# The last eight parts of an FFT convolution: their constant matrices asked for early, stores moved to SyncE's queue, sums made in pairs

## The chip, the cores and the metric

The kernel runs on one core of a Trainium2 chip. The core has a matrix engine (TensorE, PE in the profile), a vector engine (VectorE, DVE), a scalar engine (ScalarE, ACT), GpSimd (POOL) and SyncE (SP), which here only issues transfers. All five run their own instruction lists and wait for each other through semaphores; transfers are issued from the lists of SP, ACT and POOL and carried out by 16 DMA engines. The metric is the device time of one execution in microseconds (us), lower is better.

## What is computed

The reference is one block of a network over 2048 positions and 640 channels, in float32. Cut to what matters:

```python
h = _layernorm(x) * (1 + ca) + sa
x = x + ga * ssm_conv(h)          # y = irfft(rfft(K) * rfft(h)) + h * Dskip, K from A, B, C, dt
h = _layernorm(x) * (1 + cb) + sb
x = x + gb * ((_silu(h @ w1) * (h @ w3)) @ w2)
```

The first half is a long convolution, done through a Fourier transform that is itself written as matrix products. The second half is an MLP with 1728 hidden channels, done in fp32r matrix products that are most of the kernel's time.

## The kernel before

**Stages.** The convolution's kernel `K` is made in 40 steps of 16 channels, and the transform runs beside it. The 640 channels are five chunks of 128 (`NDC`), and each chunk has eight parts (`g` = 0 to 7). I number the parts 0 to 39 over the chunks, n = 8*chunk + g, so that the last chunk is parts 32 to 39. One part goes through six pieces:

- `stage2`: 8 matmuls of the input and of `K` (tile `uk`) with a constant matrix `s2`, into a PSUM tile `p2`. The profile drops digits at the end of a name, so this is the group p<-uk,s. Two PSUM tiles serve the last parts by turns.
- `k_copy`: ACT copies the half of `p2` that belongs to `K` into `kc`.
- `products`: two DVE multiplications, T<-p,kc and p<-p,kc.
- `sums`: two DVE instructions, a subtraction and an addition of 128x256 each, into `Y` (two buffers).
- `inverse1`: 8 matmuls with a second constant matrix `i1` into a PSUM tile `pz`, the group pz<-Y,i. One `pz` holds two parts.
- `z_store` (`z_last` in the last chunk): ACT copies `pz` into a tile `zt`, and two transfers bring it to `zs` in DRAM.

**Constants.** `s2` and `i1` are different for each g, 256 KB each, and are loaded anew for every part into two buffers each (`stage2_load`, `inverse1_load`, on SP). A load can therefore start only when the part two before it has been through its matmuls.

**Order.** Up to step 40 the order of every engine is written out by hand (`FRONT`, `ROUND`). What is left, from the copy `kc` of part 32 on, is done by a plain loop, `for tk in range(NS + 1, LAG + 8 * NDC + 2)`, whose steps ask for stage2, k_copy and products and sums of one part and inverse1 and z_store of the part before it. There the order is not fixed by hand: the framework's scheduler orders each engine's list by what it expects to be ready. Only ACT's copies keep the order of the program (`acopy`), so that ACT's list is always kc(n), zt(n-1), kc(n+1), zt(n).

**What comes next.** `z_last` stores the last chunk part by part. While the last parts run, POOL loads `z` tiles back for the first four MLP row tiles (`z_load`, and the loads in `z_last` after parts 37 and 39), `x_part` turns them with small matmuls (py<-A,i) and adds the residual; after part 39 `x_first` finishes them, with 10 and 18 matmuls on an idle tile around it (`keep_warm`) that keep PE busy. Then the MLP starts. The MLP's hidden tiles are `h_tile()`, 18 places of 128x512 in the pool `xp`, which is opened in the space of the tables (`tabs`) after step 41. When the first weights of the MLP and two tiles of x are asked for hangs on `i1_last`, the last load of an `i1`.

Of the kernel before, what the change touches and what calls it, by code (L numbers as in the profile page):

```python
# [9 lines left out]
F32 = mybir.dt.float32  # L10
F32R = mybir.dt.float32r
I32 = mybir.dt.int32
AF = mybir.ActivationFunctionType
OP = mybir.AluOpType
# [3 lines left out]
P = 128  # L18
# [5 lines left out]
NDC = D // DC  # L24
SD = 16
SPC = DC // SD
NS = D // SD
EB = 4
NT = L // P
KD = D // P  # L30
# [83 lines left out]
def tile_kernel(ctx: ExitStack, tc: tile.TileContext, a):  # L114
    nc = tc.nc
    V, S, G, PE = nc.vector, nc.scalar, nc.gpsimd, nc.tensor
# [3 lines left out]
    zs = dram.tile([NDC, NB, 2, NA, DC], F32, name="zs")  # L120
# [15 lines left out]
    V, S, G, PE, Q = (InOrder(tc, e, (front,)) for e in (nc.vector, nc.scalar, nc.gpsimd, nc.tensor, nc.sync))  # L136

    def keep(ins):

        return tc.keep_in_program_order(ins) if in_order[0] else ins  # L140
# [5 lines left out]
    def acopy(out, in_):  # L146
        return tc.keep_in_program_order(S.copy(out, in_))
# [30 lines left out]
    tabs = ExitStack()  # L178
# [482 lines left out]

    ahead = {}

    def stage2_load(g):

        s2 = fp.tile([P, 4, P], F32, name="s2")
        nc.sync.dma_start(s2, a["s2"][:, g * 4:g * 4 + 4, :])
        return s2

    def inverse1_load(g):  # L670

        i1 = fp.tile([P, 2, 2, P], F32, name="i1")
        i1_last[0] = nc.sync.dma_start(i1, a["i1"][:, g * 2:g * 2 + 2])
        return i1

# [33 lines left out]
    def sums(ch, g):  # L709
        T, T2 = Pq.pop((ch, g))  # L710
        Y = fp.tile([P, 2, 2, DC], F32, name="Y")
        keep(V.tensor_tensor(Y[:, :, 0, :], T[:, :, 0, :], T2[:, :, 0, :], op=OP.subtract))
        last_sum[0] = keep(V.tensor_tensor(Y[:, :, 1, :], T[:, :, 1, :], T2[:, :, 1, :], op=OP.add))
        Yq[ch, g] = Y

    last_sum = [None]
# [34 lines left out]
    def z_last(g):  # L751

        zt = fp.tile([P, 8, DC], F32, name="zt", bufs=2)[:, :4]
        acopy(zt.rearrange("p (i r) d -> p r i d", r=2), Zq[NDC - 1][:, :, (g % 2) * 2:(g % 2) * 2 + 2, :])
        for c in range(2):
            (nc.sync if g == 7 and c else S).dma_start(zs[NDC - 1, :, c, g * 4:g * 4 + 4], zt[c * 64:c * 64 + 64])
        if g in (5, 7):
            fs = (0, 24) if g == 5 else (24, 32)
            for j in range(4):
                for c in range(2):  # L760
                    r = slice(c * 32 + fs[0], c * 32 + fs[1])
                    ins = (nc.gpsimd if g == 5 else S if c else nc.sync).dma_start(
                        early[j][1][64 + r.start:64 + r.stop, :, 2 * DC:], zsv[r, 4 * j:4 * j + 4, NDC - 1])
                    if g == 5 or c == 0:
                        zlast[g == 5] = ins


    def z_load(z, j, ks, q=nc.sync, b0=0):

        nb = z.shape[1]  # L770
        for k in ks:
            hh = int(k > 1)
            kk = k - 2 * hh
            q.dma_start(z[hh * 64:hh * 64 + 64, :, kk * DC:kk * DC + DC],
                        zsv[:, 4 * j + b0:4 * j + b0 + nb, k])

    def x_tile():
        return xp.tile([P, D], F32, name="xm", bufs=6)

    def h_tile():  # L780
        return xp.tile([P, 512], F32, name="h", bufs=18)
# [16 lines left out]
    early = []  # L798
# [6 lines left out]
    def x_part(j, after):  # L805

        x, z, st = early[j]
        py = [psS.tile([P, 512], F32, name="py", tag=t, bufs=1) for t in ("pk", "pb")]
        with tc.issue_after(after.ins):
            for b in range(4):  # L810
                for hh in range(2):
                    r, c = slice(hh * 64, hh * 64 + 64), slice(b * NA, b * NA + NA)
                    PE.matmul(py[hh][c, :2 * DC], i2[r], z[r, b, :2 * DC], start=True, stop=True,
                              tile_position=(r.start, c.start))
        S.copy(x[:, 512:], xe[j][:, 512:])
        for hh in range(2):
            h = slice(hh * 256, hh * 256 + 256)
            V.tensor_tensor(x[:, h], py[hh][:, :256], xe[j][:, h], op=OP.add)
        for k in range(4):
            V.bn_stats(st[:, k, :], x[:, k * P:(k + 1) * P])  # L820


    LAG = SPC + 2

    def conv_part(fn):
# [3 lines left out]
             "PQ": lambda k: exp_slow((k,)), "XQ": slow, "E1": real1, "E2": real2, "A1": imag1, "A2": imag2,  # L829
             "kg": kgen, "K": k1evac, "pt": k_stage1, "uk": k_out}  # L830
    conv = {"st": conv_part(stage2), "kc": conv_part(k_copy), "T": conv_part(products), "Y": conv_part(sums),
            "iv": conv_part(inverse1), "zt": conv_part(z_store)}
    by_two = ("PH", "AB", "CO", "SI")
    done = set()

    def do(name, k):

        lo, hi = (LAG, LAG + 8 * NDC) if name in conv else (0, NS)
        if name in by_two and k % 2:
            return None  # L840
        if front[0]:
            assert (name, k) not in done and lo <= k < hi, (name, k)
        if (name, k) in done or not lo <= k < hi or (name == "zt" and k % 2 == 0 and k < LAG + 8 * NDC - 8):
            return None
        done.add((name, k))
        return (conv if name in conv else parts)[name](k)
# [5 lines left out]
    fp = None  # L852
    xp = None
    first_w = dict.fromkeys(("wg", "wu"))

    def pre_end():

        pre.close()
        return ssm.enter_context(tc.tile_pool(name="fp", bufs=2, side="right", reuse_waits="tile"))
# [52 lines left out]
    for word in FRONT:  # L912
        name, k = word[:2].rstrip("+"), int(word[len(word[:2].rstrip("+")):])
        if name == "CL":
            fp = pre_end()
# [25 lines left out]
    for rnd in range(NS // EB):  # L941
        if 2 <= rnd < 7:
            late_load(rnd - 2)
        for word in ROUND:
            name, k = word[:2].rstrip("+-"), EB * rnd + int(word[len(word[:2].rstrip("+-")):])
# [11 lines left out]
    in_order[0] = False  # L957

    for tk in range(NS + 1, LAG + 8 * NDC + 2):
        do("st", tk)  # L960
        do("kc", tk)
        last = do("iv", tk - 1)
        do("zt", tk - 1)
        do("T", tk)
        do("Y", tk)
        if tk == NS + 1:
            tabs.close()
            xp = ctx.enter_context(tc.tile_pool(name="xp", bufs=2))
            idle = xp.tile([P, 512], F32R, name="idle", bufs=1)
            G.memset(idle.bitcast(F32), 0.0)  # L970
            for j in range(4):
                early[j] = (x_tile(), early[j][1], xp.tile([P, KD, 6], F32, name="st5", bufs=4))
        i = tk - 1 - LAG - 8 * NDC + 8
        if 0 <= i < 8:
            if i < 4:
                z_load(early[i][1], i, (3,), q=nc.gpsimd)
            for j in ((), (), (), (), (0,), (1,), (), (2, 3))[i]:
                x_part(j, last)
# [18 lines left out]
    V, S, G, PE = (InOrder(tc, e, (in_order,)) for e in (nc.vector, nc.scalar, nc.gpsimd, nc.tensor))  # L997
# [166 lines left out]
    ahead = {(0, n): w for n, w in first_w.items()}  # L1164
# [410 lines left out]
```

## Time and profile before

| | us |
|---|---|
| median of 3 runs | 952.9 (952.22 to 956.66) |
| the profiled execution | 954.98 |
| its span, first to last instruction | 952.8 |
| PE busy | 879.5 (92%) |
| DVE busy | 710.2 (75%) |
| ACT busy | 538.9 (57%) |
| stretch of the last eight parts: stage2 of part 32 starts, inverse1 of part 39 ends | 343.57 to 377.47 |

The profile's times count from the start of its span. PE, DVE, ACT, POOL are engines; SPq, ACTq and POOLq are instructions that issue a transfer. L108 is the line of the helper that records nearly all instructions, so groups are told apart by the tiles. A matmul of fp32 data is shown twice, so the 8 matmuls of a stage2 or an inverse1 are x16. The clock that PE was granted is 1.00 at full speed and 0.50 at half.

### The profile page before, as it was taken

How to read it: one execution, taken by the hardware profiler on the slowest of the kernel's cores; microseconds unless marked ns; L12 is line 12 of the kernel's file. 1: busy time of each engine (PE TensorE's matmuls, PEld its weight loads, DVE VectorE, ACT ScalarE, POOL GpSimd, SP SyncE). 2: the span in 40 equal slices, each digit the busy share in tenths (PEclk: the TensorE clock that was granted, in tenths of full speed). 3: DMA queues.
4: the chain of work that ended last, by engine and by line, in shares of the span. 5: the costliest groups of instructions: out<-in, count | busy, mean ns of one | idle time of the engine just before them, and what ended most of it. 6: DMA issues, size and time to landing. Idle time of an engine off the chain costs nothing.

```text
span 952.8 us, 20012 instructions
## 1 busy us (share of the span) xinstructions
PE 879.5 (92%) x7950; PEld 669.8 (70%) x7950; DVE 710.2 (75%) x1232; ACT 538.9 (57%) x737; POOL 269.0 (28%) x293
## 2 busy tenths in 40 slices
PE   3687979999998898999999999999999999999997
PEld 2453556666666664678888887578888888888786
DVE  5999979999999957577666665587976666664674
ACT  5877989999999632455333332466533333333332
POOL 3423345444544211133222201230242222200241
PEclk9867579999999998899999999999999999999999
DMA  8455397667675877782111116955321311123252
GB/s 267 149 170 195 153 230 208 170 180 195 195 224 153 231 219 255 203 262 83 42 56 56 56 62 191 248 199 171 126 70 55 111 56 56 56 82 98 97 189 87
DMA packets 104048, 140.68 MB, mean 148 GB/s; under 512 B 21044, under 2 KB 63156, under 8 KB 103956
## 3 DMA queue, kind: packets, MB, share of 16 engines
q1 hardware_dynamic: 93172, 113.58, 39.8%
q10 hardware_dynamic: 8480, 18.09, 5.9%
q0 software_dynamic: 2304, 7.74, 2.6%
q8 instruction: 62, 1.02, 0.4%
q14 instruction: 30, 0.25, 0.1%
HBM read 107.92 MB, written 31.46 MB: 146 GB/s over the span
## 4 chain that ended last, share of the span: by engine, by line
PE 68%; DVE 13%; ACT 7%; DMA 4%; SPq 3%; issue 3%; POOL 1%; ACTq 0%; DVEq 0%; POOLq 0%
PE ps L108 49%; PE p L108 6%; SPq L108 3%; PE pz L108 3%; PE pt L108 3%; PE pk L108 2%; PE pa L108 2%; DVE uk L108 2%; DVE u L108 2%; DVE st L108 2%; DVE E L108 1%; DVE A L108 1%; PE pu L108 1%; PE pm L108 1%; ACT A L108 1%
## 5 line engine op out<-in xcount | busy, mean ns | idle before, releaser
L108 DVE TENSOR_TENSOR s<-ps,s 128x512 f32<-128x512 f32 x138 | 94.8, 687 | 82.3 <-PE ps L108 81.6
L108 ACT CAST gh<-rw 128x640 fp32r<-128x640 f32 x87 | 63.3, 728 | 128.0 <-PE ps L108 86.4
L108 DVE TENSOR_TENSOR gl<-rw,gh 128x640 fp32r<-128x640 f32 x87 | 78.7, 904 | 69.1 <-ACT gh L108 69.1
L108 POOL TENSOR_TENSOR S<-rw 128x256 f32<-128x256 f32 x46 | 36.3, 791 | 234.3 <-DVE S0l L108 158.5
L108 PE MATMUL p<-uk,s 128*64 128x256 f32 x640 | 81.1, 397 | 16.3 <-DVE Y L108 4.0
L108 PE MATMUL ps<-xA,gh 128*128 128x512 f32 x280 | 87.6, 391 | 0.4 <-ACT xA L108 0.4
L108 PE MATMUL ps<-gh,uh 128*128 128x512 f32 x224 | 87.6, 391 | 0.0
L108 POOL TENSOR_TENSOR ph<-thi,iota 128x1376 int32<-128x1376 int32 x20 | 51.1, 2554 | 129.1 <-DVE A L108 114.0
L108 PE MATMUL ps<-gl,uh 128*128 128x512 f32 x224 | 87.3, 390 | 0.0
L108 PE MATMUL ps<-gh,ul 128*128 128x512 f32 x208 | 81.1, 390 | 0.0
L108 DVE TENSOR_TENSOR E<-A,cs 128x1024 f32<-128x1024 f32 (+1 forms) x80 | 76.5, 973 | 0.0
L108 PEld LDWEIGHTS p<-uk,s 128*64 128x64 f32 x640 | 46.6, 140 | 40.4 <-issue 7.7
L108 ACT ACTIVATE A<-pa 128x1024 f32<-128x1024 f32 (+1 forms) x80 | 64.6, 815 | 14.7 <-PE pa L108 14.6
L108 PEld LDWEIGHTS ps<-xA,gh 128*128 128x128 f32 x280 | 52.3, 188 | 12.9 <-ACT xA L108 1.0
L108 DVE TENSOR_TENSOR A<-A,ph 128x1024 f32<-128x1024 f32 x40 | 54.1, 1357 | 0.9
L108 PE MATMUL ps<-xA,gl 128*128 128x512 f32 x140 | 54.5, 390 | 0.0
L108 PE MATMUL pt<-s,K 128*64 128x128 f32 x640 | 47.4, 294 | 3.4 <-ACT uk L108 3.3
L108 PE MATMUL pz<-Y,i 64*128 64x128 f32 x640 | 47.3, 288 | 3.4 <-DVE T L108 1.8
L108 PEld LDWEIGHTS pz<-Y,i 64*128 64x128 f32 x640 | 39.6, 190 | 14.3 <-issue 8.4
L108 PE MATMUL pa<-r,lx 32*128 32x512 f32 (+1 forms) x160 | 34.5, 480 | 15.9 <-DVE u L108 9.0
L108 PEld LDWEIGHTS ps<-gl,uh 128*128 128x128 f32 x224 | 42.1, 188 | 9.0
L108 PEld LDWEIGHTS ps<-gh,uh 128*128 128x128 f32 x224 | 42.1, 188 | 8.9 <-DVE h L108 0.2
(211 smaller groups left out, 2181.1 us busy)
## 6 DMA issues: line engine op xcount, KB each, us to landing
rw<-in_w_dram ACTq DMA_DIRECT2D x44, 320.0 KB
us<-u SPq DMA_DIRECT2D x16, 640.0 KB
s<-in_s_dram SPq DMA_DIRECT2D x40, 256.0 KB
i<-in_i_dram SPq DMA_DIRECT2D x40, 256.0 KB
rw<-in_wg_dram SPq DMA_DIRECT2D x31, 320.0 KB
rw<-in_wu_dram SPq DMA_DIRECT2D x28, 320.0 KB
uk<-us SPq DMA_DIRECT2D x32, 256.0 KB
zs<-zt SPq DMA_DIRECT2D x32, 256.0 KB
```

Source lines behind the costliest of these rows:

```text
L108: ins = fn(*args, **kw)
```

## The change

It touches the loop for the last parts and four functions.

- At the loop's first step (`tk == NS + 1`) the tables' space is closed and `xp` is opened before the step's pieces rather than after them, and right there `s2` and `i1` of parts 33 to 39 are asked for, 14 loads in a row on SP, into 14 of the 18 places of `h`. Part 32 keeps its own `s2` and `i1` tiles; its `i1` is asked for where `inverse1` needs it, two steps of the loop later.
- In the last chunk the `zs` stores of parts 32 to 37 go out on SP's queue and no longer on ACT's.
- In the last chunk `sums` makes four instructions of 128x128 rather than two of 128x256: subtraction and addition for the first pair of frequencies, then for the second.

```diff
-    def stage2_load(g):
+    def stage2_load(g, room=None):
...
-        s2 = fp.tile([P, 4, P], F32, name="s2")
+        s2 = fp.tile([P, 4, P], F32, name="s2") if room is None else room.rearrange("p (f m) -> p f m", f=4)
         nc.sync.dma_start(s2, a["s2"][:, g * 4:g * 4 + 4, :])
...
-    def inverse1_load(g):
+    def inverse1_load(g, room=None):
...
-        i1 = fp.tile([P, 2, 2, P], F32, name="i1")
+        i1 = (fp.tile([P, 2, 2, P], F32, name="i1") if room is None else
+              room.rearrange("p (q c m) -> p q c m", q=2, c=2))
         i1_last[0] = nc.sync.dma_start(i1, a["i1"][:, g * 2:g * 2 + 2])
...
-        keep(V.tensor_tensor(Y[:, :, 0, :], T[:, :, 0, :], T2[:, :, 0, :], op=OP.subtract))
-        last_sum[0] = keep(V.tensor_tensor(Y[:, :, 1, :], T[:, :, 1, :], T2[:, :, 1, :], op=OP.add))
+        for pi in (slice(0, 1), slice(1, 2)) if ch * 8 + g + LAG > NS + 1 else (slice(0, 2),):
+            keep(V.tensor_tensor(Y[:, pi, 0, :], T[:, pi, 0, :], T2[:, pi, 0, :], op=OP.subtract))
+            last_sum[0] = keep(V.tensor_tensor(Y[:, pi, 1, :], T[:, pi, 1, :], T2[:, pi, 1, :], op=OP.add))
...
-            (nc.sync if g == 7 and c else S).dma_start(zs[NDC - 1, :, c, g * 4:g * 4 + 4], zt[c * 64:c * 64 + 64])
+            (nc.sync if g < 6 or g == 7 and c else S).dma_start(zs[NDC - 1, :, c, g * 4:g * 4 + 4], zt[c * 64:c * 64 + 64])
...
     for tk in range(NS + 1, LAG + 8 * NDC + 2):
+        if tk == NS + 1:
+            tabs.close()
+            xp = ctx.enter_context(tc.tile_pool(name="xp", bufs=2))
+            idle = xp.tile([P, 512], F32R, name="idle", bufs=1)
+            G.memset(idle.bitcast(F32), 0.0)
+            for g in range(1, 8):
+                ahead[NDC - 1, g, "s2"] = stage2_load(g, h_tile())
+                ahead[NDC - 1, g, "i1"] = inverse1_load(g, h_tile())
+            for j in range(4):
+                early[j] = (x_tile(), early[j][1], xp.tile([P, KD, 6], F32, name="st5", bufs=4))
         do("st", tk)
         do("kc", tk)
         last = do("iv", tk - 1)
         do("zt", tk - 1)
         do("T", tk)
         do("Y", tk)
-        if tk == NS + 1:
-            tabs.close()
...
```

How the engines' lists move is shown at two places. Outside of this stretch all five lists are the same as before.

SP, from the last loads that both kernels share on; `s_4458` is `s2` of part 32, `uk<-us` the last input loads of part 38 and 39, the first `zs<-zt 64x1024 x2` the stores of parts 28 and 29, the second those of parts 30 and 31. Before:

```order
L667 DMA s_4458<-in_s_dram 128x512
L673 DMA i_4469<-in_i_dram 128x512
L747 DMA zs<-zt 64x1024 x2
L659 DMA uk<-us 64x8x128 x2
L667 DMA s_4505<-in_s_dram 128x512
L673 DMA i_4518<-in_i_dram 128x512
L667 DMA s_4540<-in_s_dram 128x512
L747 DMA zs<-zt 64x1024 x2
L673 DMA i_4553<-in_i_dram 128x512
```

And in the changed kernel, at the end of the 14 loads into places of `h`, of which the last two are shown:

```order
L667 DMA h<-in_s_dram 128x512
L674 DMA h<-in_i_dram 128x512
L749 DMA zs<-zt 64x1024 x2
L674 DMA i_4546<-in_i_dram 128x512
L793 DMA rw<-in_wg_dram 128x640
L793 DMA rw<-in_wu_dram 128x640
L992 DMA xm<-in_x_dram 128x640 x2
L758 DMA zs<-zt 64x512 x13
```

Before, `i_4518`, the `i1` of part 32, is second after the `uk` loads. In the changed kernel it is `i_4546` and stands behind 14 loads and two stores. The first weights and x tiles of the MLP (`rw`, `xm`) now stand right behind it and ahead of the `zs` stores of the last chunk.

PE, from the inverse of part 31 (`i_4469`) on; `p_...` is the stage2 of the next part each time. Before:

```order
L108 MATMUL pz<-Y,i_4469 128x128 x8
L108 MATMUL p_4507<-uk,s_4505 64x256 x8
L108 MATMUL pz<-Y,i_4518 128x128 x8
L108 MATMUL p_4542<-uk,s_4540 64x256 x8
L108 MATMUL pz<-Y,i_4553 128x128 x8
L108 MATMUL p_4576<-uk,s_4574 64x256 x8
L108 MATMUL pz<-Y,i_4587 128x128 x8
L108 MATMUL p_4611<-uk,s_4609 64x256 x8
```

After:

```order
L108 MATMUL pz<-Y,i_4469 128x128 x8
L108 MATMUL p_4535<-uk,h 64x256 x8
L108 MATMUL p_4570<-uk,h 64x256 x8
L108 MATMUL p_4602<-uk,h 64x256 x8
L108 MATMUL pz<-Y,i_4546 128x128 x8
L108 MATMUL pz<-Y,h 128x128 x16
L108 MATMUL p_4635<-uk,h 64x256 x8
L108 MATMUL pz<-Y,h 128x128 x8
```

Before, stage2 and inverse1 take turns. In the changed kernel the stage2 of parts 33, 34 and 35 come first, then the inverses of 32, 33 and 34, then stage2 of 36; from there they take turns again, and the inverses of 38 and 39 end the stretch together. On ACT the copies stand as before, kc(33), zt(32), kc(34), zt(33), without the 12 store issues between them.

More of the change, by code (lines that the diff above doesn't have):

```diff
@@ L965, in tile_kernel @@
         do("Y", tk)
-        if tk == NS + 1:
-            tabs.close()
[L968 to L972, printed above, removed]
         i = tk - 1 - LAG - 8 * NDC + 8
```

## The prediction

> **What bounds the kernel now.** I first asked the windows and PE's own list in order of time for the stretch that the change touches. All other lists are unchanged, so only this stretch and what it hands on can move the total. PE's list, with start, duration, and in brackets the idle time before and what ended it:
>
> ```profile
> 343.57 1.95 PE L108 MATMUL p<-uk,s 128*64 128x256 f32 x16
> 345.45 1.16 PE L108 MATMUL pz<-Y,i 64*128 64x128 f32 x16
> 348.59 3.39 PE L108 MATMUL p<-uk,s 128*64 128x256 f32 x16 [1.98 <-DMA s<-in_s_dram]
> 351.90 1.36 PE L108 MATMUL pz<-Y,i 64*128 64x128 f32 x16
> 353.19 1.95 PE L108 MATMUL p<-uk,s 128*64 128x256 f32 x16
> 355.07 1.16 PE L108 MATMUL pz<-Y,i 64*128 64x128 f32 x16
> 356.16 1.95 PE L108 MATMUL p<-uk,s 128*64 128x256 f32 x16
> 359.95 1.16 PE L108 MATMUL pz<-Y,i 64*128 64x128 f32 x16 [1.84 <-DVE T L108]
> 361.04 1.95 PE L108 MATMUL p<-uk,s 128*64 128x256 f32 x16
> ...
> 375.72 1.75 PE L108 MATMUL pz<-Y,i 64*128 64x128 f32 x16 [1.55 <-DVE Y L108]
> 377.41 1.10 PE L108 MATMUL py<-A,i 64*32 64x256 f32 x16
> ```
>
> The row at 343.57 is stage2 of part 32, the one at 375.72 the inverse of part 39, which the next row cuts off at 377.4. In this stretch PE is the engine that sets the pace, with three holes: 1.98 us for the constants of part 33, 1.84 us ahead of the inverse of part 34, 1.55 us at the end for the last sums. Eight parts at 1.88 + 1.09 (start to start) would be 23.8 us, and they take 33.9. So there is something to win, at most the holes and the slow part 33, some 7 us of 953.
>
> The chain of work that ended last passes through all of it, and says what the first two holes are:
>
> ```profile
> 342.92 1.01 SPq L659
> ...
> 343.98 4.47 DMA s<-in_s_dram
> 348.45 0.14 issue
> 348.59 3.39 PE p L108 x16
> 351.97 1.32 PE pz L108 x16
> ...
> 354.49 1.72 ACTq L108
> ...
> 366.00 2.37 DMA s<-in_s_dram
> ```
>
> The constants of part 33, asked for at 343.98, land at 348.45, 4.47 us later; the same load at 366.00 takes 2.37. The difference is the queue: the `uk` loads were issued on it just before, and go first. And ACT stands 1.72 us in the issue of one store at 354.49 before it may copy kc(34). The change takes away this wait and makes the loads of parts 34 to 39 early.
>
> **The change, part by part.**
>
> *The 14 loads.* All are issued on one queue from 343.98 on, where the first load of this kind is issued now. The first one is still `s2` of part 33, behind the same `uk` loads: it lands at 348.45 as now, and hole one stays. What is new is who stands behind: 13 loads, the two stores of parts 30 and 31, and only then `i1` of part 32, each 256 KB. That is the sixteenth transfer after the first, 16 x 262144 bytes = 4.19 MB. What the queue moves when it is full, by the windows (last figure GB/s; before it the DMA engines' share and PE's clock):
>
> ```profile
> 89.00:90.00 1.00, 1.00 (x72) 0.91 (x68) 0.97 (x4) 1.00 (x3) 0.37 (x1) 1.00 1.09 439
> 346.00:348.00 2.00, 0.61 (x12) 0.42 (x8) 1.71 (x3) 1.21 (x2) 0.00 (x0) 1.00 1.10 279
> 347.00:349.00 2.00, 0.41 (x4) 0.40 (x6) 1.40 (x3) 0.67 (x1) 0.00 (x0) 0.98 1.06 349
> 348.00:350.00 2.00, 1.41 (x9) 1.02 (x11) 0.44 (x2) 0.00 (x0) 0.00 (x0) 0.73 1.08 312
> 350.00:352.00 2.00, 2.00 (x12) 0.99 (x8) 0.00 (x0) 0.00 (x0) 0.00 (x0) 0.50 0.77 258
> 358.00:360.00 2.00, 0.16 (x4) 0.08 (x2) 1.84 (x5) 0.58 (x1) 0.00 (x0) 1.00 1.03 347
> ```
>
> The stretch 347 to 349 is exactly such loads back to back, so I take 347 GB/s: 4.19 / 0.347 = 12.1 us, and `i1` of part 32 lands at 348.45 + 12.1 = **360.6**. Bounds: 439 GB/s, the most that I found anywhere (with other, longer rows), gives 9.6 us and 358.0; 279 gives 15.0 and 363.5. The loads' own issue does not matter: one takes 0.33 us where it waits for nothing, against 0.76 for its 256 KB.
>
> ```profile
> 345.56 0.33 SPq L667 DMA_DIRECT2D s<-in_s_dram  x1
> ...
> 357.41 1.10 ACTq L108 DMA_DIRECT2D zs<-zt  x2
> ```
>  Today this `i1` is issued second, and the inverse of part 32 runs at 351.90.
>
> [...]
>
> *PE's list.* It now has stage2 of 33, 34 and 35 ahead of that inverse. Part 33 ends at 351.9 as now, 34 at 353.8, and 35, which needs the PSUM tile that the sums of part 33 leave at about 354.8, ends at 356.7. Then PE waits from 356.7 to 360.6: 3.9 us. Nothing behind the inverse can pass it. And behind that stand others: ACT's list has zt(32) ahead of kc(34), so the copy, the products and the sums of part 34 wait too. The prices of these steps:
>
> ```profile
> 353.31 0.59 ACT L108 COPY zt<-pz 128x512 f32<-128x512 f32 x1 [0.67 <-PE pz L108]
> ...
> 356.92 0.69 DVE L108 TENSOR_TENSOR T<-p,kc 128x512 f32<-128x512 f32 x1 [2.04 <-ACT kc L108]
> 357.65 0.70 DVE L108 TENSOR_TENSOR p<-p,kc 128x512 f32<-128x512 f32 x1
> 358.38 0.75 DVE L108 TENSOR_TENSOR Y<-T,p 128x256 f32<-128x256 f32 x2
> ...
> 358.61 0.58 ACT L108 COPY kc<-p 128x512 f32<-128x512 f32 x1 [1.23 <-DVE p L108]
> ...
> 388.37 0.22 DVE L108 TENSOR_TENSOR xm<-ps,xm 128x128 f32<-128x128 f32 x1
> ```
>
> From the landing L: inverse 32 to L + 1.1, zt(32) to 1.75, kc(34) to 2.35, T and p (0.73 each, start to start) to 3.85, and the sums. A sum of 128x128 is not in this trace; 0.22 us is a DVE instruction of that size, and half of 0.37 is 0.19, so four take 0.8 to 0.9 rather than 0.75, the first pair 0.4. Inverse 34 starts at L + 4.35 and ends, with the second pair's sums in time, at L + 5.5. There stage2 of part 36 starts: 360.6 + 5.5 = 366.1, against 361.04 now, **+5.1 us**.
>
> *From part 36 to the end.* Now it is 377.4 - 361.04 = 16.4 us, PE with its turns, the chain copy, products, sums at the end. The loads are no longer waited for, but they are not waited for now either after part 33, except by the chain's piece at 366.00. What the pairs give is here: the last inverse starts on the first pair, 0.75 - 0.4 = 0.35 us sooner, and the finer sums cost 0.1 each on DVE, which has slack until the last. I take **-0.4**.
>
> *Stores on SP.* ACT loses 12 issues, 0.55 us each (the pair at 357.41 above), which matters where it delays kc: at parts 34 and 35, inside the stretch already counted as lost. SP's stores stand behind 1.3 MB of weights and x that now come early; zt(34) needs the place that the stores of part 32 leave, 1.28 MB / 0.347 = 3.7 us after L, plus the store: about L + 6 to 7, when inverse 34 (L + 5.5) and then part 36 (to L + 7.4) are through. kc(36) behind it is delayed by nothing to 0.5 us. I take 0. The early weights are first used long after 377 and cost nothing.
>
> *PE's clock.* This is a term that the lists do not show. After the hole of 1.98 us the windows above have the clock at 0.73 and 0.50, and the stage2 in it takes 3.39 us where others take 1.95. After a hole at 374 to 375.7 the same, and it stays at half over 376 to 384:
>
> ```profile
> 376.00:380.00 4.00, 3.43 (x48) 1.80 (x45) 1.40 (x6) 0.58 (x1) 3.79 (x7) 0.53 0.78 272
> 380.00:384.00 4.00, 3.02 (x21) 2.06 (x7) 2.35 (x8) 1.35 (x2) 0.85 (x2) 0.50 0.40 122
> 384.00:388.00 4.00, 4.00 (x40) 2.73 (x40) 1.50 (x6) 0.00 (x0) 0.00 (x0) 0.69 0.00 0
> ```
>
> The new wait is twice as long as the first, so I expect half clock behind it until PE has been busy for some us without a gap, and inverse 34's own wait (L + 2.2 to 4.35) keeps it from that. An inverse at half clock takes 1.75 us (the row at 375.72) instead of 1.16. On the path stand inverse 32 (+0.6), inverse 34 (+0.6) and half of stage2 36 (+0.7 of 1.4): **+1.9**. Bounds: 0, if part 35 ends late enough, and +4, if half clock lasts until part 37.
>
> [...]
>
> *Sum.* +5.1 - 0.4 + 1.9 = **+6.6 us**. The profiled execution took 954.98 (span 952.8), so it would take 961.6; that execution lies 2.1 above the median of 952.9, and for the median I say 959.5. All that follows hangs on part 39's output in the same way as before, the loads, the idle matmuls and the MLP, and moves along.
>
> **The rivals.**
>
> *Not slower, the queue drains fast.* Speaking for it: rates above 400 GB/s do occur. With 439 GB/s the `i1` lands at 358.0, PE waits 1.3 us and keeps its clock: 358.0 + 5.5 = 363.5 against 361.04, less 0.4, gives +2.1: 955.0. If beside this the end keeps full clock, because its hole shrinks, the ten idle matmuls and the last py turns run at full speed:
>
> ```profile
> 381.49 4.61 PE L108 MATMUL ps<-idle 128*128 128x512 f32 x10 [0.98 <-DVE xm L108]
> ...
> 387.23 4.41 PE L108 MATMUL ps<-idle 128*128 128x512 f32 x18
> ```
>
> ten at the second row's pace are 2.5 us instead of 4.6, and with py about 3 us come back: 955.0 - 3 = 952. The point from which this decides is a landing before 357. Against it: the longest saturated stretch of these very loads runs at 349, and the end still has a wait for the last sums.
>
> *Faster by over 0.5%.* It needs `i1` of part 32 by 352 as now, hence an overtaking on the queue, or another 5 us in the MLP's start from the early weights. The chain shows no wait for those first weights. I see no row for it.
>
> *Worse.* 279 GB/s, because stores, POOL's loads of `z` and the early weights mix in, puts the landing at 363.5 (+2.9), and half clock until part 37 adds 2 more: +11.5, 964.4.
>
> *The change does not do what it says*, in that the loads wait for the tables' space: the idle tile, which lies in it too, is written at 342.77 on POOL after PE pt, so the space is free a microsecond before the first load's issue. This is part of the forecast.
>
> ```profile
> 342.77 0.53 POOL L108 MEMSET idle<- 128x512 f32 x1 [20.17 <-PE pt L108]
> ```
>
> **How the numbers follow.** About 0.5% (4.8 us) is what a measurement of this kernel can tell from no change. Forecast (+3 to +10, middle +6.6): 0.73. Fast queue (0 to +3): 0.15. Faster: 0.05. Worse: 0.07. Of the forecast's band some 0.13 lies below +4.8, so slower by over 0.5% is 0.60 + 0.07 = 0.67, within 0.5% is 0.15 + 0.13 = 0.28, faster 0.05. The range goes from the fast queue's +2.1 (955.0) to the worse case's +11.5 (964.4); it leaves out the faster cases and the tail beyond.
>
> **What would show it.** Right: PE has a hole of 3 to 5 us ahead of an inverse, ended by DMA i<-in_i_dram, near 356.7 to 360.6; behind it windows at clock 0.5; kc<-p of part 34 after that inverse; stage2 of 36 near 366 to 368; the last inverse ends near 383 to 385 instead of 377.4. Wrong: if `i1` of part 32 lands before 357, or stage2 and the inverses run on without that hole, or the time between part 39's inverse and the first MLP product shrinks by over 3 us.

## The result and the profile after

| | us |
|---|---|
| before, median of 7 runs | 952.9 (951.99 to 958.98) |
| after, median of 7 runs | 963.31 (960.05 to 964.93) |
| ratio after to before, 95% interval | 1.0092 [1.0064, 1.0119] |
| profiled executions, before and after | 954.98 and 964.47 |
| their spans | 952.8 and 961.1 |

The change makes the kernel about 0.9% slower, 8.8 us by the ratio. The profile after shows it in one place. TensorE's list there in order of time (start, duration, in brackets the idle time before and what ended it), from stage2 of part 32 to the end of the stretch and what comes behind it:

```profile
343.90 1.95 PE L108 MATMUL p<-uk,s 128*64 128x256 f32 x16
...
349.43 3.68 PE L108 MATMUL p<-uk,h 128*64 128x256 f32 x32 [2.48 <-DMA h<-in_s_dram]
354.52 1.95 PE L108 MATMUL p<-uk,h 128*64 128x256 f32 x16 [1.41 <-issue]
361.19 2.08 PE L108 MATMUL pz<-Y,i 64*128 64x128 f32 x16 [4.73 <-DMA i<-in_i_dram]
363.95 2.08 PE L108 MATMUL pz<-Y,h 64*128 64x128 f32 x16 [0.68 <-ACT zt L108]
366.76 2.08 PE L108 MATMUL pz<-Y,h 64*128 64x128 f32 x16 [0.73 <-ACT zt L108]
368.76 3.68 PE L108 MATMUL p<-uk,h 128*64 128x256 f32 x16
372.37 1.16 PE L108 MATMUL pz<-Y,h 64*128 64x128 f32 x16
...
385.34 1.16 PE L108 MATMUL pz<-Y,h 64*128 64x128 f32 x16 [1.71 <-issue]
...
389.63 2.53 PE L108 MATMUL ps<-idle 128*128 128x512 f32 x10 [0.98 <-DVE xm L108]
...
399.83 2.67 PE L108 MATMUL ps<-ident,T 128*128 128x128 f32 x20 [0.64 <-ACT T L108]
```

The row at 361.19 is inverse 32. It starts 17.3 us after stage2 of part 32 began; before, that was 8.3 us (351.90 - 343.57). It and the two inverses behind it take 2.08 us each and stage2 of part 36 takes 3.68, where 1.16 and 1.95 are the times at full clock. The chain of waits names what stands ahead of that inverse:

```profile
344.40 4.89 DMA h<-in_s_dram
...
349.31 5.69 DMA h<-in_s_dram
...
355.06 5.99 DMA i<-in_i_dram
...
361.19 2.10 PE pz L108 x16
```

From 344.4 to 361.06 SyncE's queue always has loads in flight, and the one that TensorE needs was asked for behind the 14 early loads and two stores. The windows show the clock (the third figure from the end, then the busy share of the DMA engines and GB/s):

```profile
352.00:356.00 4.00, 2.59 (x25) 1.78 (x23) 2.27 (x6) 0.04 (x1) 0.00 (x0) 1.00 1.06 400
356.00:360.00 4.00, 0.47 (x5) 0.01 (x1) 0.00 (x0) 0.00 (x0) 0.00 (x0) 0.84 1.05 371
360.00:364.00 4.00, 2.13 (x18) 1.87 (x18) 0.00 (x0) 0.69 (x2) 2.43 (x4) 0.50 1.01 330
...
368.00:372.00 4.00, 4.00 (x24) 2.25 (x22) 1.53 (x5) 0.58 (x1) 0.00 (x0) 0.50 0.56 121
372.00:376.00 4.00, 4.00 (x46) 2.69 (x44) 2.27 (x6) 1.67 (x3) 0.00 (x0) 0.96 0.15 33
```

So the account of the profiled execution, before against after, is in two pieces that I use for every run below. The **stretch**, from the start of part 32's stage2 to the end of the last inverse, was 33.9 us (343.57 to 377.47) and is 42.6 (343.90 to 386.50). The **tail**, from there to the first transposes of the MLP's input, was 14.8 us (to 392.26) and is 13.3: the ten idle matmuls in it run at full clock (1.00 from 388 to 392), 2.53 us and not 4.61, and two waits of 0.52 and 0.66 us for the exchange through DRAM take part of that back. Together +7.2 us, and with the start 0.33 us later and 0.7 in the MLP the span's +8.3.

### The profile page after: what moved, and what is told of

It is laid out like the page before. It is cut to its first block, busy times and chain, and to the rows that moved or that the text cites. A ratio compares the mean times of both kernels' runs of the same rounds, so it can differ in the third digit from the quotient of the medians.

```text
span 961.1 us, 20025 instructions
## 1 busy us (share of the span) xinstructions
PE 878.8 (91%) x7950; PEld 669.1 (70%) x7950; DVE 712.5 (74%) x1248; ACT 539.6 (56%) x737; POOL 268.9 (28%) x293
## 4 chain that ended last, share of the span: by engine, by line
PE 66%; DVE 15%; DMA 7%; ACT 6%; SPq 3%; issue 2%; POOL 0%; DVEq 0%; ACTq 0%
PE ps L108 50%; PE p L108 6%; PE pz L108 3%; SPq L108 3%; PE pt L108 2%; DVE E L108 2%; DVE uk L108 2%; DVE A L108 2%; PE pk L108 2%; DVE u L108 2%; ACT cs L108 2%; PE pa L108 1%; DMA h<-in_s_dram 1%; ACT A L108 1%; DVE st L108 1%
## 5 line engine op out<-in xcount | busy, mean ns | idle before, releaser
L108 PE MATMUL p<-uk,s 128*64 128x256 f32 x528 | 68.7, 405 | 12.3 <-DVE Y L108 3.6
L108 ACT ACTIVATE A<-pa 128x1024 f32<-128x1024 f32 (+1 forms) x80 | 64.6, 815 | 13.3 <-PE pa L108 13.1
L108 PEld LDWEIGHTS p<-uk,s 128*64 128x64 f32 x528 | 39.5, 143 | 32.7 <-issue 5.7
L108 DVE TENSOR_TENSOR T<-p,kc 128x512 f32<-128x512 f32 x40 | 27.5, 687 | 29.9 <-ACT kc L108 29.8
L108 PEld LDWEIGHTS pt<-s,K 128*64 128x64 f32 x640 | 36.5, 143 | 14.0 <-ACT uk L108 7.1
```

Source lines behind the costliest of these rows:

```text
L108: ins = fn(*args, **kw)
```

## The experiments

Theory one: the loss is the place of one load, `i1` of part 32, behind 14 loads that are needed later; the half clock follows from the wait for it. Rivals: the loss lies in TensorE's new order (three stage2 ahead of inverse 32), in the stores on SyncE's queue or the finer sums, or in bandwidth, so that no order of the requests would help. Stretch and tail are of one profiled execution each. In these 14 executions the stretch begins anywhere from 341.4 to 345.4 us, so whole spans of single executions are not compared, and a few tenths of a us in a stretch or tail show nothing. The ratio is against runs of the kernel before on the same chip (their medians are 955.3 to 956.4 us, so times are compared by the ratio):

| kernel | stretch | tail | ratio, 95% interval |
|---|---|---|---|
| before | 33.9 | 14.8 | |
| after | 42.6 | 13.3 | 1.0092 [1.0064, 1.0119] |
| urgent load first | 35.4 | 13.6 | 1.0003 [0.9985, 1.0021] |
| early loads alone | 42.6 | 13.4 | 1.0097 [1.0074, 1.0120] |
| stores and pairs, no early loads | 32.6 | 17.0 | 1.0026 [1.0009, 1.0042] |
| TensorE kept warm | 39.6 | 14.6 | 1.0084 [1.0061, 1.0107] |
| three parts early | 35.5 | 17.6 | 1.0033 [1.0013, 1.0053] |
| urgent load on ScalarE's queue | 36.5 | 13.3 | 1.0008 [0.9990, 1.0025] |
| urgent first, three parts early | 33.9 | 17.3 | 1.0009 [0.9989, 1.0028] |
| urgent first, stores moved | 33.6 | 13.6 | 0.9984 [0.9962, 1.0006] |
| the same, u behind | 38.9 | 13.2 | 1.0042 [1.0022, 1.0062] |
| the same, u behind, three parts early | 31.0 | 17.1 | 1.0017 [1.0002, 1.0033] |
| the same, u behind, room for z | 36.1 | 13.6 | 1.0020 [1.0001, 1.0039] |
| urgent first, room for z | 34.5 | 14.6 | 1.0010 [0.9992, 1.0028] |

**The urgent load first.** The kernel after, with one line added:

```diff
+            ahead[NDC - 1, 0, "i1"] = inverse1_load(0)
             for g in range(1, 8):
                 ahead[NDC - 1, g, "s2"] = stage2_load(g, h_tile())
```

> The change with one line more: i1 of part 32 is asked for ahead of the 14 loads. Theory (place in the queue: the loss is the wait of inverse 32 for a load that stands sixteenth): i1 of 32 lands near 349, s2 of part 33 0.8 us later than now, no wait of PE over 2.5 us in the stretch, clock full from 353 on, last inverse ends near 374 to 377, time 950 to 954, some 10 us under the change. Rival A (the early loads crowd out others wherever that i1 stands) and rival B (the z stores on SP's queue and the early weights cost it): 959 to 964, as the change.

Measured 955.88 us, ratio 1.0003: the whole loss is gone by moving one load of 256 KB, and the expected gain (to 950 to 954) is not there. With the load early, the scheduler also puts inverse 32 ahead of stage2 of part 33 again, so this run alone does not tell the load's place from TensorE's order. TensorE's list:

```profile
348.57 1.23 PE L108 MATMUL pz<-Y,i 64*128 64x128 f32 x8 [2.32 <-DMA i<-in_i_dram]
349.73 2.86 PE L108 MATMUL p<-uk,h 128*64 128x256 f32 x16
```

Inverse 32 now starts 5.4 us after stage2 of part 32 began, but the load still takes 4.9 us behind the `uk` loads, and the hole costs the clock as before (0.57 from 348 to 352; stage2 of part 33 in 2.86 us, where 1.95 is the time at full clock). ScalarE's list in order of time shows a new wait, the copies of `pz` standing for an earlier store to land (the last run below shows what it is worth):

```profile
359.94 0.58 ACT L108 COPY zt<-pz 128x512 f32<-128x512 f32 x1 [4.16 <-DMA zs<-zt]
...
366.89 0.58 ACT L108 COPY zt<-pz 128x512 f32<-128x512 f32 x1 [3.99 <-DMA zs<-zt]
...
370.63 0.58 ACT L108 COPY zt<-pz 128x512 f32<-128x512 f32 x1 [2.67 <-DMA zs<-zt]
```

The stores are on the queue that carries the 4 MB, and `zt` has two places.

**The early loads alone.** Stores back on ScalarE's queue for parts 32 to 37, two sums of 128x256:

```diff
-            (nc.sync if g < 6 or g == 7 and c else S).dma_start(zs[NDC - 1, :, c, g * 4:g * 4 + 4], zt[c * 64:c * 64 + 64])
+            (nc.sync if g == 7 and c else S).dma_start(zs[NDC - 1, :, c, g * 4:g * 4 + 4], zt[c * 64:c * 64 + 64])
...
-        for pi in (slice(0, 1), slice(1, 2)) if ch * 8 + g + LAG > NS + 1 else (slice(0, 2),):
+        for pi in (slice(0, 1), slice(1, 2)) if False else (slice(0, 2),):
```

> The 14 early loads alone; stores back on ACT's queue, sums in two instructions. Theory (place in the queue): same wait for i1 of part 32, landing at 360 to 362, half clock behind it, time 961 to 965. Rival B (stores on SP behind the weights): 953 to 956.

Measured 964.3 us, ratio 1.0097, the stretch 42.6 as in the kernel after. The loads carry all of the loss:

```profile
345.37 1.95 PE L108 MATMUL p<-uk,s 128*64 128x256 f32 x16
...
351.17 8.64 PE L108 MATMUL p<-uk,h 128*64 128x256 f32 x48 [2.76 <-DMA h<-in_s_dram]
362.36 1.16 PE L108 MATMUL pz<-Y,i 64*128 64x128 f32 x16 [2.54 <-DMA i<-in_i_dram]
```

Here the clock fell before the wait (0.50 from 352 to 356): three stage2 in 8.64 us, and a wait of 2.54 rather than 4.73. Inverse 32 starts 17.0 us after stage2 of part 32 began, as in the kernel after (17.3). So the landing sets this point, whatever TensorE's clock did before it.

**Stores and pairs without the early loads.** The 14 loads are taken out of the kernel after; each part asks for its own as before.

```diff
-            for g in range(1, 8):
-                ahead[NDC - 1, g, "s2"] = stage2_load(g, h_tile())
-                ahead[NDC - 1, g, "i1"] = inverse1_load(g, h_tile())
```

> Stores on SP and sums in pairs alone, loads as before the change. Theory (place in the queue): no new wait; ACT's 1.7 us wait in a store's issue goes, time 950 to 953.5. Rival B: 957 to 963.

Measured 957.41 us, ratio 1.0026 [1.0009, 1.0042]: a small loss where I expected a small gain. The stretch is 1.3 us shorter, and the tail 2.2 us longer. TensorE's list in the tail:

```profile
384.37 0.42 PE L108 MATMUL ps<-A,i 64*32 64x128 f32 x8 [1.88 <-DMA A<-zs]
385.79 1.51 PE L108 MATMUL ps<-A,i 64*32 64x128 f32 x24 [0.99 <-DMA A<-zs]
387.22 6.73 PE L108 MATMUL ps<-idle 128*128 128x512 f32 x18
```

The exchange through DRAM is late, and the 18 idle matmuls behind the holes run at half clock for most of their time (0.50 from 388 to 392; 6.73 us, 4.38 in the kernel after). SyncE's list shows in front of it four transfers of the MLP's weights and x, 1.3 MB, of which the first row is the first; the second row, from the chain of waits, is a store of part 39 on ScalarE's queue and the time until it landed, 3.06 us in the kernel after:

```profile
372.30 0.53 SPq L793 DMA_DIRECT2D rw<-in_wg_dram  x1
...
377.49 4.83 DMA zs<-zt
```

The kernel before has the four in front of its exchange too, but asks for the first at 371.08, 6.4 us before its last inverse ends; here, behind the stores of part 37, it is 4.5 us. In the kernel after they are asked for at 355.8 to 358.1, since they hang on the last `i1` load. In the nine kernels that ask for all 14 early the tail is 13.2 to 14.6 us; in the four that have the stores on SyncE's queue and ask for the later `i1` in turn it is 17.0 to 17.6. In these four the first weights are asked for 4.4 to 4.6 us before the last inverse ends. So what the early requests do gain lies in the tail and not in the stretch; that the weights are the cause fits all these times, but no run moved them alone.

**TensorE kept warm.** The kernel after, with 16 matmuls on the idle tile between stage2 of part 35 and inverse 32, so that the wait is not idle time (`st_end` is the last matmul of the latest stage2):

```diff
+        if tk == NS + 5:
+            warm = psS.tile([P, 512], F32, name="ps", tag="pk", bufs=1)
+            with tc.issue_after(st_end[0].ins):
+                for _ in range(16):
+                    PE.matmul(warm, idle[:, :P], idle, start=True, stop=True)
```

> The change with 16 products on the idle tile between stage2 of part 35 and inverse 32, some 4 us of PE work into a free PSUM bank; nothing else differs. If half clock behind the wait is a cost of its own (in the change's trace inverses of 2.08 instead of 1.16 and a stage2 of 3.68 instead of 1.95): i1 lands at 361 as in the change, clock 1.00 behind it, stage2 of part 36 ends near 368.5 to 369.5 instead of 372.4, time 959 to 961. If only the wait counts and the clock is hidden by other engines: 962 to 964.

Measured 962.84 us, ratio 1.0084 [1.0061, 1.0107]. The wait for `i1` ends at 361.34, 16.7 us after the start of the stretch (17.3 in the kernel after), and the clock holds through the first two inverses:

```profile
356.58 3.92 PE L108 MATMUL ps<-idle 128*128 128x512 f32 x16
361.34 1.16 PE L108 MATMUL pz<-Y,i 64*128 64x128 f32 x16 [0.84 <-DMA i<-in_i_dram]
363.17 1.16 PE L108 MATMUL pz<-Y,h 64*128 64x128 f32 x16 [0.68 <-ACT zt L108]
365.56 1.94 PE L108 MATMUL pz<-Y,h 64*128 64x128 f32 x16 [1.23 <-ACT kc L108]
367.43 2.78 PE L108 MATMUL p<-uk,h 128*64 128x256 f32 x16
```

The stretch is 3.0 us shorter than in the kernel after, the tail 1.3 longer. Of the 3.0 us, 0.6 is the earlier landing; the other 2.4 are what the half clock costs at least out of the stretch's 8.7, since the clock still falls behind the hole of 1.23 us (0.72 from 364 to 368; the third inverse takes 1.94 us, stage2 of part 36 2.78). In the total the gain is not told apart from zero, since the intervals overlap: by the time it is the expectation's second case, by the stretch the first.

**Three parts early.** `range(1, 8)` becomes `range(1, 4)`; TensorE's order stays that of the kernel after, with `i1` of part 32 behind 6 loads and 2 stores.

> As the kernel after, but only the matrices of parts 33 to 35 are asked for at once (7 parts become 3; the rest is asked for in its own turn). The inverse matrix of part 32 then stands behind 6 loads and 2 stores instead of 13 and 2. By theory one (the place of that load in the queue is the cause): it lands near 354 to 355, some 6.5 us earlier than the 361.06 of the kernel after, before TensorE is through the second product of part 35 (356.5), so that TensorE waits for no inverse matrix; the third and fourth inverse keep full clock or lose it for under 2 us; stretch from part 32's second product to the last inverse 34 to 37 us (before 33.9, after 42.6); time 0.0 to 0.4% over the kernel before. By the rival (the loss lies in TensorE's new order, three second products ahead of inverse 32, or in the stores and the pairs, not in that load): the order of the products is unchanged here, the time stays 0.7 to 1.1% over the kernel before.

Measured 959.0 us, ratio 1.0033, stretch 35.5. TensorE's order is the same, there is no wait for `i1`, and two thirds of the loss are gone. So the rival of TensorE's order does not hold for the main part.

```profile
355.26 1.95 PE L108 MATMUL p<-uk,h 128*64 128x256 f32 x16 [0.94 <-PE p L108]
357.14 1.16 PE L108 MATMUL pz<-Y,i 64*128 64x128 f32 x16
358.99 1.16 PE L108 MATMUL pz<-Y,h 64*128 64x128 f32 x16 [0.69 <-ACT zt L108]
361.37 1.71 PE L108 MATMUL pz<-Y,h 64*128 64x128 f32 x16 [1.22 <-ACT kc L108]
```

When `i1` landed is not seen (no one waited for it); it was asked for at 350.27, where the kernel after asks at 355.06. What is left of the loss, 0.33%, lies in the stretch with 1.6 us and in the tail with 2.8, both against the kernel before. Whether TensorE's order has a part in the 1.6 is not shown.

**The urgent load on ScalarE's queue.** Asked for behind the same 14 loads in the program, but on another queue:

```diff
-        i1_last[0] = nc.sync.dma_start(i1, a["i1"][:, g * 2:g * 2 + 2])
+        i1_last[0] = (S if q else nc.sync).dma_start(i1, a["i1"][:, g * 2:g * 2 + 2])
```

> As the kernel after, but the inverse matrix of part 32 is asked for on ScalarE's queue; the fourteen early loads stay on SyncE's ahead of it. By theory one (the wait is the place in one queue, served in order): on a queue of its own the load passes the fourteen, lands by 350 to 352, and the run looks like the one with that load asked for first: the long wait for it is gone, stretch 34 to 37 us, time within 0.2% of the kernel before. By the rival (the transfers share one bandwidth, so that whatever is asked for after 4 MB lands after 4 MB, on any queue): it lands at 358 to 361, the wait for it stays over 2 us, and the time stays 0.6 to 1.1% over the kernel before.

Measured 956.25 us, ratio 1.0008. The issue on ScalarE's list, and TensorE's list:

```profile
344.03 0.36 ACTq L108 DMA_DIRECT2D i<-in_i_dram  x1
```

```profile
348.82 0.68 PE L108 MATMUL pz<-Y,i 64*128 64x128 f32 x6 [1.87 <-DVE Y L108]
350.71 3.20 PE L108 MATMUL p<-uk,h 128*64 128x256 f32 x16 [1.22 <-DMA h<-in_s_dram]
```

The load is there by 348.82, when the sums end TensorE's wait. The run says less than I meant it to: ScalarE reached this issue at 344.03, 0.56 us before SyncE issued the first of the 14 at 344.59 (which landed 5.99 us later), so the load was ahead of them in time as well. It shows that the request need not stand on SyncE's queue, and again that its early place is all that is needed. Whether a later request on a second queue would overtake loads that already wait is open.

**Urgent load first, three parts early.** Both edits at once.

> Both at once: the inverse matrix of part 32 is asked for first, and only the matrices of parts 33 to 35 behind it. In the run with that load first and all fourteen behind it, ScalarE's evictions of z waited 10.8 us in three places for the z stores, which stood behind the loads. By the theory that these stores were held up by the queue of loads: with 2 MB fewer ahead of them the z stores land some 6 us sooner, those three waits come to under 4 us in all, the stretch falls from 35.4 to 32 to 34 us, and the time to 950 to 955 against a kernel before of 953 to 956 (0.1 to 0.4% faster). By the rival (the evictions wait for the stores' own way, the first weights of the MLP that are asked for early, not for the fourteen): the waits stay near 10 us and the time within 0.2% of the kernel before.

Measured 956.42 us, ratio 1.0009. In ScalarE's list no copy waits for a store any more, as the first theory said, and the stretch is back at 33.9 (32 to 34 was expected, and a time of 950 to 955); but the tail is 17.3. The exchange is late again:

```profile
385.42 0.42 PE L108 MATMUL ps<-A,i 64*32 64x128 f32 x8 [2.32 <-DMA A<-zs]
```

What the one gains the other gives back, and the time is not told apart from that of the kernel before.

**Stores moved.** The urgent load first, the 14 behind it, the stores of parts 30 and 31 on GpSimd's queue, and the first weights tied to an inverse near the end:

```diff
+            (nc.gpsimd if (ch, g) == (NDC - 2, 7) else nc.sync).dma_start(zs[ch, ...
+        if tk == LAG + 8 * NDC - 1:
+            i1_last[0] = last
```

> The inverse matrix of part 32 first, all fourteen loads behind it, but the z stores of part 31 on GpSimd's queue, and the MLP's first weights held back until the last inverse of the convolution has issued. By theory one (in the run with that load first the gain was lost to z stores behind 4 MB of loads and weights): the eviction of part 33 waits under 1 us for a store (4.16 before), those of the later parts under 2 us each; the stretch is 31 to 33 us; the weights then land later, and the MLP's first products may wait 1 to 3 us for them; time 0.3% faster to the same as the kernel before. By the rival (stores and loads share the bandwidth, and it is bytes that hold the stores up): the waits of the evictions stay over 8 us in sum, and the time is the same as the kernel before or up to 0.4% slower by the late weights.

Measured 954.4 us, ratio 0.9984 [0.9962, 1.0006]. The tie did not hold the weights until the last inverse; it moved them between the stores (asked for at 356.69 to 364.72), so that half of this expectation was not put to a test. Copies still waited for stores, 3.24 and 0.60 us, with a hole of 0.36 us in TensorE's list behind the longer; under 2 us each was expected, and a stretch of 31 to 33. It is the fastest of the kernels here, and not told apart from the kernel before.

**The same, u behind.** What is left at the head of the stretch is the hole of 2.46 us ahead of inverse 32. The last quarter of `uk`, first used by part 38, goes behind the loads of part 35:

```diff
-        if g % 2 == 1 and ch + 1 < NDC:
+        if g % 2 == 1 and ch + 1 < NDC and (ch, g) != (NDC - 2, 7):
...
+                if g == 3:
+                    u_load(NDC - 1, 3)
```

> The kernel with the inverse matrix of part 32 first, part 31's z stores on GpSimd's queue and the MLP's first weights held back (0.9984 of the kernel before, interval 0.9962 to 1.0006), with one more edit: the last quarter of u, which part 38 is the first to use, is asked for behind the matrices of part 35 instead of ahead of all early loads. If the remaining hole ahead of inverse 32 (2.46 us, and the half clock after it, one second product of 3.61 instead of 1.95 us) comes from that matrix standing behind the two u loads: it is asked for about 1.5 us earlier against part 32's second product, the hole falls under 1 us, full clock holds, the stretch from part 32's second product to the last inverse falls from 33.6 to 30 to 32 us, and the time to 0.3 to 0.6% under the kernel before. If the hole comes from the landing itself (some 5 us from issue whatever stands ahead): hole 1.5 to 2.5 us, stretch 33 to 34, time 0 to 0.3% under the kernel before. A third: the second product of part 38 waits for its u, which now lands after 2.6 MB of matrices; then a DMA wait for uk stands ahead of it.

Measured 959.42 us, ratio 1.0042, against what I expected. The hole did go; two others came. TensorE's list, and ScalarE's:

```profile
348.59 1.16 PE L108 MATMUL pz<-Y,i 64*128 64x128 f32 x16
350.46 1.95 PE L108 MATMUL p<-uk,h 128*64 128x256 f32 x16 [0.71 <-DMA h<-in_s_dram]
...
358.12 2.08 PE L108 MATMUL pz<-Y,h 64*128 64x128 f32 x16 [2.75 <-ACT zt L108]
...
366.34 1.16 PE L108 MATMUL pz<-Y,h 64*128 64x128 f32 x16 [1.97 <-ACT zt L108]
```

```profile
357.48 0.58 ACT L108 COPY zt<-pz 128x512 f32<-128x512 f32 x1 [4.40 <-DMA zs<-zt]
...
365.70 0.58 ACT L108 COPY zt<-pz 128x512 f32<-128x512 f32 x1 [7.15 <-DMA zs<-zt]
```

TensorE comes to the copies sooner than the stores land. The first copy's wait ends as the stores on GpSimd's queue land (a median of 7.7 us from issue to landing); the second's stores are asked for on SyncE's queue from 357.87 on, behind all early loads, and land at 365.55. Half clock follows both holes, at once behind the first (2.08) and behind one more hole of 1.15 us after the second.

**The same, u behind, three parts early.**

> The same with only the matrices of parts 33 to 35 asked for early; parts 36 to 39 ask in their own turn. If early requests for all seven parts are worth something once they stand behind the urgent load: 0.1 to 0.3% slower than the kernel with all seven (holes of 0.5 to 1.6 us ahead of the second products of parts 36 and on). If the early request of the later parts is worth nothing: the same within 0.1%.

Measured 956.95 us, ratio 1.0017, where I expected it slower than the kernel with all seven. It has the shortest stretch of all, 31.0 us, 2.9 below the kernel before, and gives 2.3 back in the tail: the weights are asked for from 368.87 on, and the windows show the DMA engines full in front of the exchange (share 0.99, 358 GB/s):

```profile
372.00:376.00 4.00, 2.75 (x48) 1.49 (x48) 2.63 (x12) 0.58 (x1) 3.90 (x7) 1.00 0.99 358
```

**Room for z.** The `zt` of parts 32 to 35 in the four free places of `h`, so that those copies wait for no store; once on the kernel with u behind (stores of part 31 back on SyncE's queue), once on the kernel with the urgent load first alone:

```diff
-        zt = fp.tile([P, 8, DC], F32, name="zt", bufs=2)[:, :4]
+        zt = (h_tile().rearrange("p (f d) -> p f d", d=DC) if g < 4 else
+              fp.tile([P, 8, DC], F32, name="zt", bufs=2))[:, :4]
```

> The kernel with the inverse matrix of part 32 first, the last quarter of u behind the matrices of part 35 and the MLP's first weights held back, part 31's z stores back on SyncE's queue; and the z tiles of parts 32 to 35 take the four places of the MLP's h tiles that the early loads leave free, so that their evictions need no earlier store to have landed. In the run without these places the holes ahead of inverses 34 and 35 were 2.75 and 1.97 us, ended by evictions that waited 4.40 and 7.15 us for stores behind 4 MB of loads. If those two waits, with the half clock behind them, were what was left of the loss: the evictions of parts 33 to 35 wait for no store, the stretch from part 32's second product to the last inverse falls from 36.0 (38.9 with the half clock of that run's end) to 29 to 32 us, and the time is 0.2 to 0.6% under the kernel before. If the stretch shrinks but the stores then land late at its end (the exchange waits for them): the tail from the last inverse to the first transposes grows from 13 to 14 us to 16 to 18, and the time is within 0.2% of the kernel before.

> As the kernel after, with two edits alone: the inverse matrix of part 32 asked for first, and the z tiles of parts 32 to 35 in the four free places of the h tiles. The run with the first edit alone had a stretch of 35.4 us with 10.8 us of evictions waiting for z stores in three places. If these waits are what turned the expected gain of that run into nothing: stretch 31 to 33 us and the time 0.1 to 0.4% under the kernel before. If they were covered by other work: stretch 34 to 36 us, time within 0.1% of the kernel before.

The first (it starts from a stretch of 38.9 us) took 957.44 us, ratio 1.0020, stretch 36.1, where I expected 29 to 32 and a gain: no copy waits for a store, and the wait turns up at the next place that needs the stores, the small matmuls `py` on the tiles that come back from `zs`:

```profile
362.73 0.62 PE L108 MATMUL py<-A,i 64*32 64x256 f32 x2
367.40 0.66 PE L108 MATMUL py<-A,i 64*32 64x256 f32 x14 [4.05 <-DMA A<-zs]
367.99 3.59 PE L108 MATMUL p<-uk,h 128*64 128x256 f32 x16
```

The second took 956.43 us, ratio 1.0010, stretch 34.5 against 35.4: the 10.8 us of waiting copies in the run with the urgent load first were nearly all covered by other work, as that expectation's second case had it.

So theory one stands for the loss. For the gain that did not come there is no single cause. Wherever the 14 loads stand, their 3.7 MB have to pass (the 4.19 MB up to `i1` took 11.8 us in the kernel after), and `uk`, the stores and what is read back from them share the queue or the DMA engines with them; in these runs each wait that I took away was followed by one behind it. Whether three parts early, with the weights kept out of the tail, would beat the kernel before was not run.

## Why the prediction was right, and where its size was off

- **The landing.** Forecast: the first `h` load lands at 348.45, the sixteenth transfer 12.1 us later, 360.6. Measured: 349.29 and 361.06, 11.8 us, in a trace whose stretch starts 0.33 us later. I took 347 GB/s for the 4.19 MB; 11.77 us make it 356. That a late request waits for the bytes ahead of it on its queue carried the forecast; it was my estimate from the 4.47 against 2.37 us. The run with that request first and the one with three parts early show it together: in the first the loss is gone, in the second, with TensorE's order as in the kernel after, two thirds of it (ratios 1.0003 and 1.0033 against 1.0092). Whether a load can overtake others that wait on its queue no run shows; that the rival "faster" would need it to was my estimate too.
- **The wait.** Forecast 3.9 us, measured 4.73. Stage2 of part 35 ended at 356.47, because the hole of 2.48 us ahead of part 33 did not cost the clock (two stage2 in 3.68 us, where before one took 3.39).
- **The chain from the landing to stage2 of part 36.** Forecast: inverse 34 starts 4.35 us after the landing at full clock. The run with three parts early, at full clock, has 4.23 from the start of inverse 32 to that of inverse 34 (361.37 - 357.14). The kernel after has 5.57.
- **The clock**, which is the term of the sum that was mis-sized. Forecast +1.9, bounds 0 to +4. Stage2 of part 36 ends 9.45 us later than before (372.44 against 362.99), 9.1 without the later start; less the 5.1 of the chain that leaves 4.0, at the upper bound. Two things were missing. I read an inverse at half clock from a row of 1.75 us in which the clock changed (0.84 from 375.7 to 376.5, 0.50 behind that); a whole one takes 2.08. And I counted inverses 32 and 34 on the path; inverse 33 stands between them, and each waits for the copy of the one before (0.68 and 0.73 us), so that at half clock three inverses in a row are the longer branch, and stage2 of part 36 runs at half clock to its end (3.68, I took half of the difference).
- **From part 36 to the last inverse.** Forecast -0.4; measured 14.06 us (372.44 to 386.50) against 14.48 (362.99 to 377.47), -0.4. The agreement is luck. The forecast had the pairs bring the last inverse forward; it starts 0.17 us later behind stage2 of part 36 than before. VectorE's last sums, before and after:

```profile
375.20 0.75 DVE L108 TENSOR_TENSOR Y<-T,p 128x256 f32<-128x256 f32 x2
...
384.95 0.88 DVE L108 TENSOR_TENSOR Y<-T,p 128x128 f32<-128x128 f32 x4
```

  The inverse follows the start of these sums by 0.39 us, where it was 0.52, but the sums start 0.30 us later behind that stage2: VectorE has no gap there from part 37 on, in either kernel, and the finer sums of parts 37 and 38 take 0.13 us more each. What shortens the piece is the last inverse itself, at full clock (1.16 us and not 1.75).
- **The tail.** I let it move along unchanged; it is 1.5 us shorter, since its idle matmuls keep full clock. The rival of the fast queue had priced this piece, at about 3 us.
- **Stores on SyncE's queue**, set at 0: in the kernel after they cost nothing that shows (1.0092 with them, 1.0097 with the early loads alone), covered by the wait. With the loads in turn, stores and pairs together cost 0.26%, by the longer tail.
- The signs listed came, two of them later than given: the hole ended by `i<-in_i_dram`, half clock behind it, `kc` of part 34 after that inverse, stage2 of part 36 at 368.76 (366 to 368 was given), the last inverse's end at 386.5 (383 to 385).

Forecast +6.6 us, measured +8.8 by the ratio; the medians are 10.4 apart (952.9 and 963.31; 959.5 was forecast). By the traces the span's +8.3 is 0.33 (start), 9.1 (to the end of stage2 of part 36), -0.4, -1.5 (tail) and some 0.7 in the MLP. The clock's term, 2.1 larger than forecast, and the tail, 1.5 smaller, are the two sizes that I had wrong; they have opposite signs, so the sum came out nearer than its terms.

## What to carry to other kernels

When loads are moved forward on a queue, look first at the request that is left in its old place: here it landed 11.8 us after the first of the early loads, with 4.19 MB asked for from the one to the other, and asking for it first took the ratio from 1.0092 to 1.0003. The order of the requests should be the order of the needs. Count on the path every instruction that a late one holds up, at the clock that holds after the wait (here 0.50, an inverse of 2.08 us and not 1.16). And look at what shares the queue or the DMA engines with a burst of early loads: here, with the urgent load first, copies waited 4.16, 3.99 and 2.67 us for stores, and with six loads behind it rather than 14 (and the weights later) none did. Read the piece behind the stretch too: of a gain of 1.3 us in the stretch all, and of one of 2.9 us 2.3, were given back there.

## What the runs showed that I had not expected

- A hole in TensorE's list of about 2 us does not always cost the clock: 1.98 us before and 2.32 with the urgent load first did (a stage2 of 3.39 and 2.86 us behind it); 2.06 without the early loads, 2.48 in the kernel after and 2.55 with three parts early did not (1.95, two in 3.68, 1.95). So the length of a hole alone does not decide here; what does is not shown.
- Once lost, the clock stayed at half in the kernel after from some 359 to 372 us (0.50 there): three inverses with gaps of 0.7 us between 361 and 369 did not bring it back; it was back after the 3.68 us of unbroken stage2 from 368.76 on (0.83 from 372 to 373, 1.00 from 373 on).
- From the eighth on, SyncE issued an early load only every 0.68 us on average (348.88, 349.31, 349.97 and so on to 352.98), where an issue takes 0.33 us: the issues seem to have stood for landings. The chain shows it for `i1` of part 32, whose issue at 355.06 comes right behind the landing of a load asked for at 349.31 (5.69 us later); `i1` itself landed 5.99 us after its issue.
